# Block transposes and 64x64 tiles in the attention part of a fused attention and MLP kernel

**The chip, the cores, the metric.** One NeuronCore of a Trainium2 chip. The metric is device time in microseconds (us) of one launch. Single runs of one kernel spread by about 2 us here. Names: PE is TensorE's matmul, PEld its weight load, DVE VectorE, ACT ScalarE, POOL GpSimd.

## The reference

Attention with a polynomial sketch, then an MLP with ELU (shapes in comments):

```python
# q, k, v: (batch 4, heads 4, seq 1088, dim 32); S1, S2: (8, 32)
def phi(x):
    a = einsum('rd,bhsd->bhsr', S1, x)
    b = einsum('rd,bhsd->bhsr', S2, x)
    return einsum('bhsi,bhsj->bhsij', a, b).reshape(..., 64)
q_p, k_p = phi(q), phi(k)
kv  = einsum('bhsf,bhsd->bhfd', k_p, v)
z   = sum(k_p, axis=2)
num = einsum('bhsf,bhfd->bhsd', q_p, kv)
den = einsum('bhsf,bhf->bhs', q_p, z)[..., None] + 1e-6
x   = (num / den) -> (4352, 128)
h   = x @ w_in                        # (128, 2048)
out = where(h > 0, h, exp(min(h, 0)) - 1) @ w_out
```

w_in, w_out, S1 and S2 come as float64; the kernel rebuilds float32 values from their words. Everything is computed in float32; a float32 matmul shows as two PE instructions.

## The kernel before

The 4352 rows are cut into 68 half tiles of 64, in groups of 8 (the last, group 8, has 4). The MLP of a group runs in 8 steps: 4 h instructions, ELU on ACT and DVE, and two steps later 4 o instructions. Groups 0 and 1 are interleaved while the weights are converted, so steps 0 to 15 are theirs; group g from 2 on starts at step 8g. In a step, PE does h, then the attention pieces planned for that step ("extras"), then o of two steps earlier. The attention of each group must be ready before its first step. Parts that matter (cuts marked):

```python
def q1(g, ...):               # sketches: queries held (128x128), sketch streamed
    for i in range(n):
        nc.tensor.matmul(p[:, i * 96:i * 96 + 96], qT[b][:, t:t + 2, :], SW[:, b])   # cut
    nc.scalar.copy(abw[g], p)                                                        # cut
def q4(g):                    # outer products, transposed 128x128 on PE
    for hh in range(2):
        ...
                nc.tensor.transpose(p[:, o:o + P], qp[g][:, r:r + 2], ident[:])
        nc.scalar.copy(qpT[g][:, 2 * hh:2 * hh + 2, :nh, :], p)
def q5(g, ...):               # times kv, tiles of 64 rows x 32 columns
    ...
    nc.tensor.matmul(xp[w][D * h:D * h + D, ...], kvS[64 * w:64 * w + 64, b, h, :],
                     qpT[g][64 * w:64 * w + 64, h, ...], tile_position=(64 * w, D * h))
def KA(b, gi):                # kv: outer products held (64 columns), v streamed (33 with the ones)
    ...
    nc.tensor.matmul(kv[64 * hp:64 * hp + 64, g2, :n], kp[:rows, j, h],
                     vt[b][:rows, h * KT + i, :], tile_position=(0, 64 * hp))        # cut
```

Of the kernel before, what the change touches and what calls it, by code (L numbers as in the profile page):

```python
# [27 lines left out]
def kernel(  # L28
# [18 lines left out]

    nc = tc.nc
# [20 lines left out]
    vt = [const.tile([P, VN + D], F32, name="v0")]  # L69
    vt += [const.tile([P, H * KT, D + 1], F32, name=f"v{b}") for b in range(1, B)]  # L70
    kT = [const.tile([FD, NT, 64], F32, name=f"kT{b}") for b in range(B)]
# [8 lines left out]
    def load_v(b, engs=(nc.sync, nc.sync)):  # L80
        for u, eng in enumerate(engs):
            t0, t1 = u * KT, min(NT, u * KT + KT)
            r = slice(64 * u, 64 * u + 64)
            src = v[b].rearrange("h (y t) d -> y h t d", t=NT)[:, :, t0:t1, :]
            if b == 0:
                eng.dma_start(vt[b][r, :VN].rearrange("p (h t d) -> p h t d", h=H, t=KT)[:, :, :t1 - t0, :], src)
            else:
                for h in range(H):
                    eng.dma_start(vt[b][r, h * KT:h * KT + t1 - t0, :D], src[:, h])
# [113 lines left out]
    for b in range(1, B):  # L203
        nc.gpsimd.memset(vt[b][:, :, D:], 1.0)
# [42 lines left out]

    Sab = const.tile([FD, H, 2 * R], F32, name="Sab")
    SW = const.tile([FD, B, H, 3, R], F32, name="SW")
    keep_warm(3)  # L250
    sps = psum.tile([P, 512], F32, name="sps", tag="aux")
# [3 lines left out]
    for b in range(B):  # L255
        nc.gpsimd.tensor_copy(SW[:, b, :, :2, :].rearrange("p h x r -> p h (x r)"), Sab[:])

# [6 lines left out]
    kvS = const.tile([P, B, H, D], F32, name="kvS")  # L264
    kv_ps, feats, zms, abps = {}, {}, {}, {}

    def KF(b, p2=None):

        p = psum.tile([P, 512], F32, name="abp", tag="aux")
        if p2 is None:  # L270
            p2 = psum.tile([P, 512], F32, name="abp2", tag="aux")
        where = [(p, 64 * i) if b or i < 4 else (p2, 64 * i - 256) for i in range(8)] + [(p2, 448)]
        for i in range(KT):
            to = where[i][0][:, where[i][1]:where[i][1] + 64]
            for u in range(2 if i + KT < NT else 1):
                nc.tensor.matmul(to[64 * u:64 * u + 64, :], kT[b][:, u * KT + i, :],  # L276
                                 Sab[:].rearrange("p h y -> p (h y)"),
                                 skip_group_check=True, tile_position=(0, 64 * u))
        abps[b] = [where[i] for i in (0, 4, 8)]

# [15 lines left out]
    def KA(b, gi):  # L296

        kp, rows = feats.pop((b, gi))
        n = 2 * D if b == 0 else D + 1
        if gi == 0:  # L300

            kv_ps[b] = psum.tile([P, 4, 2 * D], F32, name="kv", **(dict(tag="aux") if b == 1 else dict(tag="o1", bufs=1)))
        kv = kv_ps[b]
        for j, i in enumerate(KG[gi]):
            for g2 in range(2):
                for hp in range(2):
# [3 lines left out]
                                     _ap(vt[b][:rows, off:off + D], [[VN - off, 2], [1, D]]) if b == 0 else  # L310
                                     vt[b][:rows, h * KT + i, :],
# [3 lines left out]
    def KC(b):  # L315

        kv = kv_ps[b][:, :2, :D + 1]
        if b == 0:
            for hp in range(2):
                r = slice(64 * hp, 64 * hp + 64)  # L320
                nc.scalar.copy(kvz[0][r, :, hp, :], kv[r])
        else:
            kvz[b] = work.tile([P, 2, 2, D + 1], F32, name="kvz", tag="kvz")
            nc.scalar.copy(kvz[b][:, :, 0], kv)

    def KZ1(b):

        zms[b] = work.tile([P, 2, 2, R], F32, name="zm", tag="zm")
        z_ = kvz[b][:, :, :, D] if b == 0 else kvz[b][:, :, 0, D:]
        nc.gpsimd.tensor_mul(  # L330
            zms[b][:], _ap(z_, [z_.ap[1], z_.ap[2] if b == 0 else [0, 2], [0, R]]),
            _ap(zmask[:], [[0, 2], [R, 2], [1, R]]))

    def KZ2(b):
# [3 lines left out]
        nc.vector.tensor_mul(SW[:, b, :, 2, :], wps[:, :H * R].rearrange("p (h i) -> p h i", h=H),  # L338
                             _ap(bmask[:], [[1, H], [0, R]]))

    def KS(b):

        for w in range(2):
            for hp in range(2):
                nc.gpsimd.tensor_copy(kvS[64 * w:64 * w + 64, b, hp::2, :],
                                      kvz[b][64 * hp:64 * hp + 64, :, hp if b == 0 else 0, :D])
# [10 lines left out]
    def half_tile(g, i, u):  # L357
        return divmod(8 * g + (2 * i + u if g < NQ - 1 else u * qn[g] + i), NT)
# [10 lines left out]
    def q1(g, tag="aux", small=False, b_k=None):  # L369

        n = qn[g]
        p = psum.tile([P, 512], F32, name="abwp", tag=tag, bufs=2 if tag == "aux" else 1)
        for i in range(n):
            (b, t), (b1, t1) = half_tile(g, i, 0), half_tile(g, i, 1)
            if (b1, t1) == (b, t + 1) and not small:
                nc.tensor.matmul(p[:, i * 96:i * 96 + 96], qT[b][:, t:t + 2, :].rearrange("p t s -> p (t s)"),  # L376
                                 SW[:, b].rearrange("p h x r -> p (h x r)"), skip_group_check=True)
                continue
            for u, (b, t) in enumerate(((b, t), (b1, t1))):
                nc.tensor.matmul(p[64 * u:64 * u + 64, i * 96:i * 96 + 96], qT[b][:, t, :],  # L380
                                 SW[:, b].rearrange("p h x r -> p (h x r)"),
                                 skip_group_check=True, tile_position=(0, 64 * u))
        if b_k is not None:
            KF(b_k, p)

        abw[g] = work.tile([P, H * 4, 3 * R], F32, name="abw", tag="abw", bufs=2)
        nc.scalar.copy(abw[g][:, :H * n, :].rearrange("p (h t) y -> p h t y", h=H),  # L387
                       p[:, :n * 96].rearrange("p (t h y) -> p h t y", t=n, h=H))
        if b_k is not None:
            KF_out(b_k)  # L390

    def q2(g, parts=1):
        m = H * qn[g]
        x = abw[g][:, :m, :]
        pw = pws[g % 2]
        nc.vector.tensor_mul(pw[:, :m, :R], x[:, :, R:2 * R], x[:, :, 2 * R:])
# [15 lines left out]
    def q1_first():  # L412
        p = psum.tile([P, 512], F32, name="abqp", tag="aux")
        for i in range(4):
            for u in range(2):
                b, t = half_tile(0, i, u)
# [29 lines left out]
    def q5_first(xps):  # L446
# [21 lines left out]
        for tt in range(2):  # L468
# [4 lines left out]
            if tt == 0:  # L473
                q1(1)

    def q4(g):

        nh = qn[g] // 2
        qpT[g] = work.tile([P, H, 2, P], F32, name="qpT", tag="qpT", bufs=2)
        for hh in range(2):  # L480
            p = psum.tile([P, 512], F32, name="qtp", tag="aux")
            for h2 in range(2):
                for m in range(nh):
                    o = (h2 * nh + m) * P
                    r = (2 * hh + h2) * qn[g] + 2 * m
                    nc.tensor.transpose(p[:, o:o + P], qp[g][:, r:r + 2].rearrange("p t i j -> p (t i j)"), ident[:])  # L486
            nc.scalar.copy(qpT[g][:, 2 * hh:2 * hh + 2, :nh, :],  # L487
                           p[:, :2 * nh * P].rearrange("p (h m s) -> p h m s", h=2, m=nh))

    def q5(g, between=False):  # L490
        nh = qn[g] // 2
        xp = [psum.tile([P, 512], F32, name="xps", tag="aux") for _ in range(2)]

        parts = {0: [], 1: []}
        for w in range(2):
            for m in range(nh):
                b, b1 = (half_tile(g, 2 * m + w, u)[0] for u in range(2))
                if b != b1:
                    parts[w] += [(b, m, 1, slice(0, 64)), (b1, m, 1, slice(64, P))]
                elif parts[w] and parts[w][-1][0] == b and parts[w][-1][3] == slice(0, P):  # L500
                    parts[w][-1] = (b, parts[w][-1][1], parts[w][-1][2] + 1, slice(0, P))
                else:
                    parts[w] += [(b, m, 1, slice(0, P))]
        for h in range(H):
            for w in range(2):
                for b, m0, m, s in parts[w]:
                    nc.tensor.matmul(xp[w][D * h:D * h + D, :nh * P].rearrange("p (m s) -> p m s", s=P)[:, m0:m0 + m, s],  # L507
                                     kvS[64 * w:64 * w + 64, b, h, :], qpT[g][64 * w:64 * w + 64, h, m0:m0 + m, s],
                                     skip_group_check=True, tile_position=(64 * w, D * h))
        xg[g] = work.tile([P, 512], F32, name="xg", tag="xg", bufs=2)  # L510
        if not between:
            q5_out(g, xp)
        return xp

    def q5_out(g, xp):
        nh = qn[g] // 2
        to = xg[g][:, :2 * nh * P].rearrange("p (m w s) -> p w m s", w=2, s=P)
        nc.scalar.copy(to[:, 0], xp[0][:, :nh * P].rearrange("p (m s) -> p m s", s=P))  # L518
        nc.vector.tensor_copy(to[:, 1], xp[1][:, :nh * P].rearrange("p (m s) -> p m s", s=P))
# [72 lines left out]
    def fin_last():  # L592
# [5 lines left out]
        for u, eng in enumerate((nc.sync, nc.scalar)):  # L598
            b, t = half_tile(g, 0, u)
# [3 lines left out]
    keep_warm(2, 192)  # L603
# [7 lines left out]
    x0 = x0_eps()  # L611
# [9 lines left out]
    KS(0)  # L621
# [3 lines left out]
    RC(1)  # L625
    for c in range(2):
# [3 lines left out]
    RA(2)  # L630
    RB(2)
    q4(1)
# [3 lines left out]
    x1 = q5(1, True)  # L636
    elu_a(0, 1, 0, (0,))
    q5_out(1, x1)
    keep_warm(1)
    elu_a(0, 1, 0, (1,))  # L640
    elu_a(0, 1, 1)
# [115 lines left out]
```

## Time and profile before

| | before |
|---|---|
| median of the first 3 runs | 291.74 us (290.99 to 293.24) |
| the profiled run | 290.04 us, span of the core 288.3 us |
| busy in the span | PE 281.5, ACT 187.1, DVE 166.4, POOL 17.1 us |
| on the chain that ended last | PE 87%, of it h 36% and o 35% of the span |

PE is the bound; h and o are the MLP itself, which the change does not touch. The chain in order of time is the view to read: its pieces are spaced as the engine really moved. Its lines stand in the prediction.

### The profile page before, as it was taken

What the parts mean: (1) busy time and instruction counts of PE and PEld (TensorE: products, weight loads), DVE (VectorE), ACT (ScalarE), POOL (GpSimd) and SP (SyncE); (2) the same over time, 40 slices, a digit from 0 to 9 for tenths busy, and PEclk for the clock granted to TensorE, in tenths of its full rate; (3) what the DMA queues carried; (4) which work ended last, traced back from release to release, by engine and by line L of the source; (5) the groups of instructions that cost most, each with busy time, mean ns of one, the idle gap of its engine ahead of it and who ended that gap; (6) DMA issues with size and microseconds to landing.
All of it is one profiled execution on the core that took longest, in us unless ns stands there. A gap on an engine that the chain in (4) does not pass through costs nothing.

```text
span 288.3 us, 3955 instructions
## 1 busy us (share of the span) xinstructions
PE 281.5 (98%) x1432; PEld 147.5 (51%) x1432; DVE 166.4 (58%) x298; ACT 187.1 (65%) x357; POOL 17.1 (6%) x49
## 2 busy tenths in 40 slices
PE   7999999999999999999999999999999999999994
PEld 5864355445544745454444554445445544444694
DVE  5897999794864483546344443563442654354442
ACT  2468787567584665646776658665766676668682
POOL 3100003533000101000000000000000000000000
PEclk9999999999999999999999999999999999999999
DMA  6997993200004000002001000020002000100020
GB/s 175 338 276 189 201 227 35 77 0 0 2 1 68 7 0 3 0 6 35 0 0 23 13 2 0 2 35 2 0 0 36 2 2 0 25 11 0 7 32 18
DMA packets 37282, 13.36 MB, mean 46 GB/s; under 512 B 31760, under 2 KB 35472, under 8 KB 37264
## 3 DMA queue, kind: packets, MB, share of 16 engines
q1 hardware_dynamic: 36752, 12.66, 19.7%
q10 hardware_dynamic: 512, 0.46, 0.5%
q8 instruction: 11, 0.18, 0.3%
q14 instruction: 7, 0.06, 0.1%
HBM read 10.88 MB, written 2.23 MB: 45 GB/s over the span
## 4 chain that ended last, share of the span: by engine, by line
PE 87%; DVE 5%; DMA 2%; ACT 2%; POOL 1%; SPq 1%; issue 1%; POOLq 0%; DVEq 0%; ACTq 0%
PE h L529 36%; PE o L566 35%; PE kv L309 3%; PE ol L589 2%; PE xps L507 2%; PE qtp L486 2%; DMA v<-in_v_dram 2%; PE abwp L376 1%; DVE gg L553 1%; PE abp L276 1%; PE abwp L380 1%; ACT e L547 1%; PE x0ps L456 1%; DMA raw_s<-in_S_dram 1%; DVE raw L120 1%
## 5 line engine op out<-in xcount | busy, mean ns | idle before, releaser
L553 DVE SCALAR_TENSOR_TENSOR gg<-e,h 128x512 f32<-128x512 f32 (+1 forms) x144 | 93.1, 656 | 105.5 <-ACT e L547 105.4
L529 PE MATMUL h<-xg,W 128*128 128x512 f32 (+1 forms) x284 | 126.9, 569 | 0.6 <-DVE W L128 0.5
L566 PE MATMUL o<-gg,W 128*128 128x512 f32 x256 | 121.9, 598 | 0.0
L545 ACT ACTIVATE e<-h 128x512 f32<-128x512 f32 (+1 forms) x144 | 81.3, 565 | 34.1 <-PE h L529 30.3
L547 ACT ACTIVATE e<-e 128x512 f32<-128x512 f32 (+1 forms) x144 | 87.3, 606 | 4.5
L529 PEld LDWEIGHTS h<-xg,W 128*128 128x128 f32 x284 | 53.3, 190 | 62.9 <-issue 55.0
L566 PEld LDWEIGHTS o<-gg,W 128*128 128x128 f32 x256 | 46.6, 190 | 50.2 <-issue 48.9
L487 ACT COPY qpT<-qtp 128x512 f32<-128x512 f32 (+1 forms) x16 | 8.1, 560 | 15.5 <-PE qtp L486 15.5
L387 ACT COPY abw<-abwp 128x384 f32<-128x384 f32 (+1 forms) x8 | 3.7, 458 | 18.4 <-PE abwp L376 8.7
L261 DVE TENSOR_TENSOR kp<-ab 128x1024 f32<-128x1024 f32 (+1 forms) x12 | 12.1, 1044 | 0.1
L309 PEld LDWEIGHTS kv<-v,kp 128*64 128x64 f32 (+1 forms) x288 | 9.1, 137 | 1.7 <-ACT e L545 0.8
L309 PE MATMUL kv<-v,kp 128*64 128x33 f32 (+3 forms) x288 | 9.8, 224 | 0.0
L107 ACT ACTIVATE W<-W,ebias 128x256 uint32<-128x256 uint32 (+1 forms) x11 | 6.6, 597 | 4.8 <-DVE W L102 4.6
L407 DVE TENSOR_TENSOR qp<-an,abw 128x1024 f32<-128x1024 f32 (+1 forms) x9 | 9.3, 1047 | 0.3
L486 PEld LDWEIGHTS qtp<-ident,qp 128*128 128x128 f32 x60 | 7.1, 141 | 4.2 <-issue 4.2
L518 ACT COPY xg<-xps 128x256 f32<-128x256 f32 (+1 forms) x8 | 2.9, 359 | 9.1 <-PE xps L507 9.1
L589 PEld LDWEIGHTS ol<-W,gg 128*128 128x128 f32 x64 | 8.1, 192 | 0.3
L589 PE MATMUL ol<-W,gg 128*128 128x128 f32 x64 | 8.1, 275 | 0.0
L486 PE MATMUL qtp<-ident,qp 128*128 128x128 f32 x60 | 7.9, 272 | 0.0
L507 PE MATMUL xps<-qpT,kvS 64*32 64x256 f32 (+2 forms) x176 | 6.7, 316 | 0.4 <-ACT qpT L487 0.4
L125 POOL TENSOR_TENSOR raw<-raw,tiny 128x512 f32<-128x512 f32 x4 | 4.2, 1044 | 42.8 <-DVE raw L120 38.8
L507 PEld LDWEIGHTS xps<-qpT,kvS 64*32 64x32 f32 x176 | 3.2, 105 | 6.3 <-ACT e L547 5.3
(89 smaller groups left out, 129.9 us busy)
## 6 DMA issues: line engine op xcount, KB each, us to landing
raw<-in_moe_w_in_dram SPq DMA_DIRECT2D x8, 256.0 KB, 6.1
raw<-in_moe_w_out_dram SPq DMA_DIRECT2D x8, 256.0 KB, 6.5
hd_k<-in_k_dram SPq DMA_DIRECT2D x3, 544.0 KB, 6.5
hd_q<-in_q_dram SPq DMA_DIRECT2D x3, 544.0 KB, 3.8
out_dram<-ob SPq DMA_DIRECT2D x40, 32.0 KB, 1.6
v<-in_v_dram SPq DMA_DIRECT2D x12, 72.0 KB, 6.3
v<-in_v_dram SPq DMA_DIRECT2D x12, 64.0 KB, 3.3
hd_k<-in_k_dram SPq DMA_DIRECT2D x1, 288.0 KB, 3.5
```

What stands on the lines that cost most here:

```text
L261: nc.vector.tensor_mul(dst, _ap(a_, list(a_.ap[1:]) + [[0, R]]), _ap(b_, [b_.ap[1], [0, R], b_.ap[2]]))
L309: nc.tensor.matmul(kv[64 * hp:64 * hp + 64, g2, :n], kp[:rows, j, h].rearrange("p i j -> p (i j)"), _ap(vt[b][:rows, off:off + D], [[VN - ...
L407: nc.vector.tensor_mul(qp[g][:, h], _ap(a_, list(a_.ap[1:]) + [[0, R]]), _ap(b_, [b_.ap[1], [0, R], b_.ap[2]]))
L486: nc.tensor.transpose(p[:, o:o + P], qp[g][:, r:r + 2].rearrange("p t i j -> p (t i j)"), ident[:])
L487: nc.scalar.copy(qpT[g][:, 2 * hh:2 * hh + 2, :nh, :], p[:, :2 * nh * P].rearrange("p (h m s) -> p h m s", h=2, m=nh))
L507: nc.tensor.matmul(xp[w][D * h:D * h + D, :nh * P].rearrange("p (m s) -> p m s", s=P)[:, m0:m0 + m, s], kvS[64 * w:64 * w + 64, b, h, :], ...
L529: nc.tensor.matmul(hs[g, cp][c][:, :n], W[:, cp, c * P:c * P + P], xg[g][:, :n])
L545: nc.scalar.activation(e, hs[g, cp][c][:, :n], RELU, scale=-1.0)
L547: nc.scalar.activation(e, e, EXP, scale=-1.0)
L553: nc.vector.scalar_tensor_tensor(gs[g, cp][:, c, :n], es[g, cp][:, c, :n], -1.0, hs[g, cp][c][:, :n], op0=ADD, op1=MAX)
L566: nc.tensor.matmul(ops[g][:, :n], W[:, cp, (2 + c) * P:(3 + c) * P], gg[:, c, :n], start=(first and c == 0), stop=(last and c == 1))
L589: nc.tensor.matmul(ops[g][i][:], gg[:, c, i * P:i * P + P], W[:, cp, (2 + c) * P:(3 + c) * P], start=(first and c == 0), stop=(last and c ...
```

## The change

The intent is to spend less PE time on attention in groups 2 to 8 and in the keys of batches 1 to 3. The sketch is held and the queries streamed, in four 64x64 tiles; transposes of 32x32 blocks on DVE replace 128x128 transposes on PE; q5 of one group and q1 of the next share one visit. On the key side v is held (32 columns) and the outer products streamed, four heads on four column tiles. z comes from a product of the two sketches. Cut to its core:

```diff
+    def KA_late(b):
+        for i in range(KT):
+            for h in range(H):
+                nc.tensor.matmul(kv[32 * h:32 * h + 32, :R * R], vt[b][...], kp[i // 5][...],
+                                 tile_position=(0, 32 * h), ...)
+            nc.tensor.matmul(kv[c:c + 32, R * R:R * R + H * R], ab[:, 0, i], ab[:, 1, i],
+                             tile_position=(0, c), ...)
...
+    def q1(g, ps):
+        for e in range(2):
+            for g2 in range(2):
+                    nc.tensor.matmul(ps[g2][64 * e:64 * e + 64, 256 + 64 * k:...], SWp[r, b], qT[b][r, t:t + m, :],
+                                     tile_position=(64 * g2, 64 * e), ...)
+    def q1_out(g):
+            nc.vector.transpose(abw[g][...], ps[g2][:, 256:256 + 32 * n])
...
+    def q4(g):
+        nc.vector.transpose(qpT[g][...], qp[g][...])
+    def q5(g, ps):
+        for f in range(2):
+            for g2 in range(2):
+                for e in range(2):
+                        nc.tensor.matmul(ps[e][64 * g2:64 * g2 + 64, ...], kvp[r, b, f, g2], qpT[g][r, ..., f, :],
+                                         tile_position=(64 * e, 64 * g2), ...)
...
-    keep_warm(2, 192)
+    x0 = x0_eps()              # moved ahead of the first key work
...
+            ((3, 5, (6, 7), 8, 10, 9), (11, 12, (13, 14), 19, 20, 21), (17, 18, (20, 21), 22, 24, 25)), 1):
+    # steps of: transpose of k, sketch, two outer products, kv, z, transpose of q
```

## The prediction

> **What bounds the kernel now.** I read the page's first two parts, then the stretches between chosen times, then the chain that ended last in order of time, then the groups by shape, and last the vector engine's own order of time.
>
> ```profile
> PE 281.5 (98%) x1432; PEld 147.5 (51%) x1432; DVE 166.4 (58%) x298; ACT 187.1 (65%) x357; POOL 17.1 (6%) x49
> ...
> PE   7999999999999999999999999999999999999994
> ...
> DVE  5897999794864483546344443563442654354442
> ```
>
> ```profile
> 28.00:46.00 18.00, 17.45 (x71) 7.63 (x70) 17.62 (x32) 14.65 (x29) 2.40 (x2) 1.00 0.97 191
> ...
> 160.00:260.00 100.00, 100.00 (x346) 46.27 (x346) 47.17 (x79) 68.35 (x123) 0.00 (x0) 1.00 0.06 9
> ```
>
> TensorE is busy throughout. In the stretches the columns are length, then busy time (and instructions) of PE, PEld, DVE, ACT and POOL. From 160 us on only PE is full. From 28 to 46 us DVE is full too (17.62 of 18.00 us), because the weights are converted there. So a PE instruction saved late is saved time; one saved early may meet DVE. "Busy" alone doesn't say what an attention block costs, as ends are modelled; the chain does, since each piece there is time from one start to the next:
>
> ```profile
> 92.89 0.81 PE abwp L380 x16
> 93.70 0.93 PE abp L276 x32
> 94.74 2.19 PE kv L309 x71
> 96.94 1.91 PE o L566 x4
> 98.85 1.72 PE h L529 x4
> ...
> 104.22 0.88 PE qtp L486 x8
> 105.10 1.72 PE o L566 x4
> 106.81 1.72 PE h L529 x4
> 108.53 0.59 PE xps L507 x16
> 109.12 2.34 PE kv L309 x72
> 111.47 1.91 PE o L566 x4
> ```
>
> A step of the main loop is four h and four o instructions, 3.44 us. Between them stand the extras: abwp projects the queries, qtp transposes their outer products, xps multiplies by kv, abp and kv are the key side. An o after a block of small tiles takes 1.91 us, 0.19 more than the plain 1.72; after qtp (full 128x128 array) it takes 1.72. The main matmuls are not touched, so the question is what the extras sum to, and whether the new chain on DVE arrives in time.
>
> **What the Trainium skill says.**
> - "TensorE: Matmul & The Clock Gate", Part 3 (packing small matmuls): matmuls in different tiles of the array run together, starts about 4 ns apart. The trace agrees where each tile gets few instructions: the 16 xps instructions (64x32 tiles, 256 columns) took 0.59 us. Two such passes on one tile are 427 ns (half of the 1.72/4 = 0.43 us of a 512-column instruction, twice); 0.16 is filling.
> - The same page, the section on LDWEIGHTS: the load time goes with the columns, P/1.2 ns: 53 ns for 64, 27 for 32. The trace fits: 8 abwp instructions with 128-column loads took 0.86 us, 108 ns each, though their 96 columns stream in 80. The kv instructions (64-column loads, 33 columns streamed, two tiles) took 2.34/72 = 32.5 ns, 65 per tile: nearer the load than the 27 ns of stream.
> - "TensorEngine Tiling (Array Packing)", Key Properties: changing the tiling mode drains the engine. The 0.19 us on the next o is this, as far as this trace shows.
> - The first page again, on the issue gap: starts never fall below about 25 ns. That would hurt many-instruction blocks. The trace is undecided: 24 xps instructions at 141.12 us took 0.61 us (25 ns each), yet 16 cannot be told from the tile limit.
>
> **The change, part by part.**
>
> *Queries, groups 2 to 8.* Before: abwp on PE, copy on ACT, qtp on PE (8 transposes) with two ACT copies, xps, two copies. After: q1 holds the sketch (64x64) and streams the queries, 8 instructions on four tiles; a DVE transpose of 32x32 blocks brings it back; the qtp transposes become one DVE transpose; q5 is 16 instructions of 256 columns on four tiles; q5 of one group and q1 of the next share one visit. Per tile q1 has two passes, 427 ns, q5 four, 853; with 0.16 of filling and 0.19 of drain a visit is 1.63 us. Boundary groups, cut in more pieces, add about 0.5 in all.
> Before, from the chain, a plain group is 0.86 + 0.03 + 0.87 + 0.59 + 0.19 = 2.54 us. All seven groups, read off the chain: abwp 5.6, qtp 5.7, xps 5.0, ten drains 1.9, so 18.2. After: six visits 9.8, less 0.2 for the short last q1, plus the lone first q1 (0.43 + 0.16 + 0.19 = 0.78), the lone last q5 (0.78) and 0.5: 11.7. Saved 6.5.
>
> *Keys of batches 1 to 3.* Before: abp 1.20 + 2 x 0.93 = 3.1, kv 2.34 + 2.19 + 2.34 = 6.9, z matmuls 3 x 0.13 = 0.4 us; with two drains not shared with a query block, 10.8. After, the sketch matmul is 16 instructions of 288 columns on eight tiles, two passes per tile: 0.48 + 0.16 + 0.19 = 0.83 each, 2.5. The outer products are streamed (64 columns, 53 ns) against v held (32 columns), four heads on four tiles, 90 instructions: per row block two passes of some 58 to 66 ns on each tile and a z piece of 27 to 60, so 145 to 190 ns, nine times, plus 0.15: near 1.5 us, 4.9 for three with two unshared drains. I choose 1.5 rather than the 2.4 that a 25 ns floor would make. The z product and two more transposes cost 0.45 each, 1.35. Sum 8.75; saved 2.0.
>
> PE extras: 29.0 to 20.5, **minus 8.5 us**.
>
> *The start.* The eps product (1.08 us on the chain before kv) moves ahead into idle PE time. But the first outer product of the queries ends on DVE only at 11.46 us and the transposes after it hardly move: I give 0.1, and 0.1 for the earlier copy of the second group: minus 0.2. The fewer v transfers (2 per batch instead of 8) win nothing: no DMA wait but 0.4 us of q and 0.6 of the sketches is listed.
>
> *New work on DVE.* ACT loses two 0.59 copies and one of 0.48 per group and takes one of 0.37 from DVE; ACT was not the bound. DVE gains per group a 1024-element transpose (1.2 us by the 1.31 of the 1088-element ones) and two PSUM transposes of 256 (0.45 each). After step 24 DVE has half of its time free; it costs nothing. At step 13, though, work heaps up:
>
> ```profile
> 70.55 0.28 DVE L396 TENSOR_TENSOR pw<-abw 128x128 f32<-128x128 f32 x1
> 70.87 0.30 DVE L398 TENSOR_REDUCE den<-pw 128x16 f32<-128x144 f32 x1
> 71.21 0.25 DVE L399 RECIPROCAL den<-den 128x16 f32<-128x16 f32 x1
> 71.50 0.29 DVE L401 TENSOR_TENSOR an<-abw,den 128x128 f32<-128x128 f32 x1
> 71.82 1.23 DVE L407 TENSOR_TENSOR qp<-an,abw 128x1024 f32<-128x1024 f32 x1
> 72.96 1.22 DVE L261 TENSOR_TENSOR kp<-ab 128x1024 f32<-128x1024 f32 x1
> ```
>
> These were steps apart from the key work. Now step 13 gives DVE a key outer product of 1280 elements (1.6, scaled from the 1.22), two gg (1.2), two transposes (0.9) and the chain above up to qp (2.4 to the start of the next): 6.0 us against a PE step of 4.2. Step 14 adds 1.2 + 1.2 and the transpose of qp (1.2) in 3.44. Following it from the start of h in step 13: qp ends near 7.1, the second key product 8.4, gg 9.6, the transpose 10.8; PE reaches q5 at 4.2 + 3.44 + 1.72 = 9.4. **A wait of about 1.5 us** in step 15, once.
>
> In steps 5 to 8 DVE takes on two transposes of 288 (0.9) but the key products come in other steps; by the same walk gg stays inside the slack that four h buffers give. I count no loss there.
>
> Sum: 291.74 - 8.5 - 0.2 + 1.5 = 284.5. I put **284.0 us**, because the walk to step 15 lets nothing overlap on DVE, where the trace has starts up to 0.1 us before the end of the one ahead.
>
> **Rivals.**
> 1. *Instruction issue takes over on PE.* Kv becomes 90 instructions instead of 72; at 25 to 28 ns each it takes 2.25 to 2.6 us and saves nothing. For: the 24 xps instructions at 25 ns each and 40 of group 6 in 1.12 us (28 each). Against: the 16 loads of a plain xps start within 0.2 us. It would add 3 us: 287.
> 2. *DVE becomes the bound.* Some 1.7 us more DVE work per group, and steps 2 to 9 are full. If every DVE microsecond added before step 16 (about 5) turned into PE waiting, the gain would shrink to 4 or 5 us: 287. Against: later DVE waits for ACT 105 us in all.
> 3. *No wait at step 15* and no drains between q5 and q1: 282, or 281 with kv at 1.2 us.
> 4. *The four 64x64 tiles don't run together* (eight and two tiles do in the trace, four nowhere): a visit would grow by over 2 us and the kernel be slower. Unlikely.
>
> **Range and chances.** The kv duration (1.2 to 2.5 us, three times) and the wait at step 15 (0 to 2.5) are the two wide terms, plus the sum of drains (some 1 us): 280.5 to 287.5. Faster by over 2% means below 285.9: most of the range. Faster 0.80, same 0.19, slower 0.01.
>
> **What would show it.** The new qps blocks of a plain group should take 1.4 us and the next o 1.91; kv of a late batch 1.5 us; kfps 0.64; the chain should show one wait of PE for the DVE transpose of qp near step 15, and no wait of q5 or h later. Qtp and the copies behind it should be left for the first two groups alone. ACT busy should fall, DVE busy rise by about 15 us while PE stays full. The prediction is wrong if kv is above 2 us, if DVE holds PE up more than once, or if the four tiles serialise.

## The result

The changed kernel took 283.32 us (median of 4 runs, 282.73 to 284.6) against 291.37 us for the kernel before (4 runs with one more beside it). The ratio is 0.9724, 95% interval 0.9658 to 0.979: faster by 2.8%. A ratio here is the mean time of one kernel's fast runs over that of the other's of the same rounds, so not quite the ratio of the medians. The time was predicted 0.7 us too high.

The page of the changed kernel, busy time by engine, and PE's busy tenths in 40 slices of the span:

```profile
PE 273.7 (97%) x1348; PEld 138.4 (49%) x1348; DVE 178.7 (63%) x319; ACT 179.8 (64%) x337; POOL 20.9 (7%) x55
...
PE   8999998999979999999999999999999999999994
```

DVE rose by 12.3 us and ACT fell by 7.3. PE now shows a 7 in slice 12 (77.6 to 84.6 us): a wait that was not there. The chain of the changed kernel (start us, length us, what; the z pieces between those of kv are too short to be listed):

```profile
93.72 1.72 PE h L661 x4
95.70 0.46 PE kvl L340 x23
96.78 1.91 PE o L698 x4
...
138.58 1.08 PE qps L627 x16
139.66 0.44 PE qps L492 x8
140.10 1.91 PE o L698 x4
```

Read it by the gaps between the large pieces. h ends at 93.72 + 1.72 = 95.44 and o starts at 96.78, so the whole of kv for batch 2 took 1.34 us for its 90 instructions, 15 ns each; the old one took 2.34 for 72. A visit of the queries is 1.08 (q5) + 0.44 (q1) = 1.52 us, and the o behind it takes 1.91 as before. The qtp, abwp and xps pieces are gone after the second group.

The wait in step 15, in order of time on PE and on DVE:

```profile
75.70 1.88 PE L661 MATMUL h<-xg,W 128*128 128x512 f32 x4
79.07 1.16 PE L627 MATMUL qps<-qpT,kvp 64*64 64x64 f32 x24 [1.49 <-DVE qpT L617]
```

```profile
74.22 1.23 DVE L520 TENSOR_TENSOR qp<-an,abw 128x1024 f32<-128x1024 f32 x1
75.36 1.22 DVE L282 TENSOR_TENSOR kpl<-abk 128x1024 f32<-128x1024 f32 x1
76.50 1.28 DVE L685 SCALAR_TENSOR_TENSOR gg<-e,h 128x512 f32<-128x512 f32 x2
77.69 1.24 DVE L617 STREAM_TRANSPOSE qpT<-qp 128x1024 f32<-128x1024 f32 x1
```

The bracket says that PE was idle 1.49 us until the DVE transpose of qp ended. On DVE the pieces stand without a gap: the second key product and two gg lie between qp and its transpose.

A second wait, with DVE, POOL and PE in order of time:

```profile
44.18 1.48 DVE L282 TENSOR_TENSOR kpl<-abk 128x1280 f32<-128x1280 f32 x1
...
44.34 2.22 POOL L122 TENSOR_TENSOR raw<-raw,tiny 128x512 f32<-128x512 f32 x1 [19.23 <-DVE raw L117]
...
47.98 1.98 PE L661 MATMUL h<-xg,W 128*128 128x512 f32 x4 [1.15 <-POOL W L123]
```

POOL's first multiply (its second, 1.29 us, follows), which took 1.04 us in the kernel before, took 2.22 beside a DVE product of two SBUF tiles, and h of step 8 waited 1.15 us for the converted weights.

Last, the start. The sketches of the first keys in time order on PE, first in the profile before and then in that of the changed kernel:

```profile
6.32 1.15 PE L276 MATMUL abp<-Sab,kT 128*64 128x64 f32 x32 [0.17 <-DVE kT L237]
```

```profile
7.48 2.08 PE L298 MATMUL abp<-Sab,kT 128*64 128x64 f32 x33
```

The same instructions take nearly twice as long in the second trace, because PE still ran at its slow clock. The record of the granted clock in the trace file shows it: its first entry, full clock, stands at 4.4 us before and at 10.6 us in the changed kernel, behind these sketches. (The PEclk row of the page does not show it; what precedes the first entry is left out there.) The first h, at 16.26 us before, came at 17.81, 1.55 us later. From the first h to the end, before took 288.3 - 16.26 = 272.0 us and the changed kernel 282.1 - 17.81 = 264.3, so 7.7 less. This stretch, "from the first h", repeats to 0.1 us in five profiles of kernels that do the same from there on (264.3 each), while the first h moves between 16.5 and 18.6 us. I use it below wherever a difference is under 2 us. It still holds the tail from the last matmul to the last output. That took 3.6 to 3.7 us in these five, but 4.0 in the profiles of before, e3b and e8 and 3.5 in that of e4; e3b and e8 change nothing near the end, so I take this as a matter of the single run, whose reason I don't know. The stretch from the first h to the end of the last matmul is free of it: 268.0 us before, 260.6 in the changed kernel, 7.4 less (7.35 before rounding).

### The profile page after: what moved, and what is told of

It is laid out like the page before. It is cut to its first block, busy times and chain, and to the rows that moved or that the text cites. A ratio compares the mean times of both kernels' runs of the same rounds, so it can differ in the third digit from the quotient of the medians.

```text
span 282.1 us, 3800 instructions
## 1 busy us (share of the span) xinstructions
PE 273.7 (97%) x1348; PEld 138.4 (49%) x1348; DVE 178.7 (63%) x319; ACT 179.8 (64%) x337; POOL 20.9 (7%) x55
## 4 chain that ended last, share of the span: by engine, by line
PE 87%; DVE 8%; issue 1%; ACT 1%; POOL 1%; POOLq 0%; DVEq 0%
PE h L661 37%; PE o L698 36%; PE ol L721 3%; PE qps L627 2%; DVE gg L685 2%; PE kvl L340 1%; PE idle L221 1%; DVE kp L282 1%; PE qps L492 1%; POOL raw L122 1%; PE x0ps L569 1%; DVE raw L117 1%; PE h L668 1%; PE x0ps L554 1%; DVE W L112 1%
## 5 line engine op out<-in xcount | busy, mean ns | idle before, releaser
L627 PE MATMUL qps<-qpT,kvp 64*64 64x256 f32 (+3 forms) x136 | 7.4, 339 | 1.5 <-DVE qpT L617 1.5
L617 DVE STREAM_TRANSPOSE qpT<-qp 128x1024 f32<-128x1024 f32 (+1 forms) x7 | 8.1, 1161 | 0.0
L282 DVE TENSOR_TENSOR kpl<-abk 128x1280 f32<-128x1280 f32 (+1 forms) x6 | 8.1, 1346 | 0.0
L627 PEld LDWEIGHTS qps<-qpT,kvp 64*64 64x64 f32 x136 | 4.7, 132 | 6.6 <-issue 3.1
L502 DVE STREAM_TRANSPOSE abw<-qps 128x256 f32<-128x256 f32 (+1 forms) x14 | 5.2, 407 | 2.0 <-ACT xg L639 2.0
L117 DVE SCALAR_TENSOR_TENSOR raw<-raw 128x256 f32<-128x256 uint32 (+1 forms) x11 | 6.0, 549 | 0.3
L112 DVE SCALAR_TENSOR_TENSOR W<-raw,W 128x256 uint32<-128x256 uint32 (+1 forms) x11 | 5.9, 541 | 0.0
L705 DVE STREAM_TRANSPOSE ob<-o 128x512 f32<-128x512 f32 x8 | 5.7, 710 | 0.1
L639 ACT COPY xg<-qps 128x256 f32<-128x256 f32 x12 | 3.9, 373 | 2.8 <-PE qps L492 2.8
L123 POOL TENSOR_TENSOR W<-raw,W 128x512 f32<-128x512 f32 x4 | 5.4, 1342 | 0.3
```

What stands on the lines that cost most here:

```text
L112: nc.vector.scalar_tensor_tensor(d, hi, 0x80000000, d, op0=AND, op1=OR)
L117: nc.vector.scalar_tensor_tensor(lo.bitcast(F32), lo, 2.0 ** -32, raw[:, :, 1], op0=MUL, op1=ADD)
L282: nc.vector.tensor_mul(dst, _ap(a_, list(a_.ap[1:]) + [[0, R]]), _ap(b_, [b_.ap[1], [0, R], b_.ap[2]]))
L627: nc.tensor.matmul(ps[e][64 * g2:64 * g2 + 64, 64 * k:64 * (k + m)], kvp[r, b, f, g2].rearrange("p c d -> p (c d)"), qpT[g][r, n * g2 + 2 ...
```

## Experiments

All ran against the kernel before. Runs e0 to e3 were one call, e4, e5, e6 and e3b another, e7, e8 and e9 a third, on another chip. All gave correct results. First h to the end and to the last matmul are from the profiled run of each.

| run | median us | ratio to before | first h, us | from the first h, us | of it to the last matmul, us |
|---|---|---|---|---|---|
| e0_after (changed kernel) | 283.10 | 0.9720 | 17.82 | 264.3 | 260.6 |
| e1_lead | 284.02 | 0.9749 | 18.35 | 264.3 | 260.6 |
| e2_ko | 283.00 | 0.9711 | 18.37 | 263.1 | 259.5 |
| e3_kp7 | 282.37 | 0.9702 | 18.44 | 263.4 | 259.7 |
| e3b_nopool | 282.86 | 0.9709 | 16.59 | 263.7 | 259.7 |
| e4_oldkeys | 286.35 | 0.9838 | 17.09 | 267.1 | 263.6 |
| e5_split | 286.34 | 0.9832 | 17.82 | 266.3 | 262.7 |
| e6_dve | 283.10 | 0.9723 | 16.50 | 264.3 | 260.6 |
| e7_best | 280.94 | 0.9656 | 18.41 | 261.8 | 258.1 |
| e8_best2 | 281.36 | 0.9659 | 17.09 | 262.2 | 258.1 |
| e9_after (changed kernel) | 284.10 | 0.9753 | 18.56 | 264.3 | 260.7 |

My theory: the gain is PE time of the attention pieces, queries and keys; part is given back in two waits that DVE causes. Rivals: the gain comes from elsewhere (the start, or DVE and ACT work moved), or new limits (instruction rate, DVE) ate the rest.

### e0_after: the yardstick

No edit.

> The changed kernel again, unaltered, as the yardstick for the runs beside it. Both theories expect about 283.3 us, 0.972 of before. If the length of the lead-in (first h matmul at 17.8 us in the profile of the changed kernel, 16.26 in that of before) hangs on when TensorE's clock warms up and not on the code, this profile may show another lead-in, 1 to 1.5 us shorter, and the single times should fall in two groups about 1.5 us apart.

The six runs lay between 282.58 and 283.92 us, and the profile repeated both waits. The first h was again at 17.82. In e9 the same kernel had it at 18.56, and e6, whose start is untouched, at 16.50. The kernel before does it too: 11 runs had spans of 288.2 to 288.4 us (three) or 289.8 to 290.3 (eight), and the profile from which I predicted, 288.3, was one of the short kind. So the start differs from run to run, and one profile of each kernel must not be compared there. The clock records of the profiles go with it: full clock came at 4.4 to 4.9 us where the first h came at 16.3 to 16.6 (before, e6, e3b), at 10.3 to 10.6 where it came at 17.8 (the changed kernel, e0, e5), and at 12.6 to 13.0 where it came at 18.4 to 18.6 (e2, e3, e7, e9). In e4 and e8 it came at 4.4 and 4.6, was halved again from 7.8 and 8.0 to 11.2 and 11.4, and the first h came at 17.09.

### e1_lead: the start of the kernel before

```diff
-    keep_warm(1, 160)
...
-    x0 = x0_eps()
+    keep_warm(2, 192)
...
     q1_first()
+    x0 = x0_eps()
```

> The changed kernel with the lead-in of before: the eps product back behind the first query projection, the two idle matmuls of 192 columns back, the extra one of 160 columns gone. Theory A (the new lead-in costs time, since the early eps product keeps TensorE at its slow start longer): first h near 16.3 us instead of 17.8 and the time 1.5 us lower than the changed kernel of the same call, near 281.8. Theory B (it is the phase of the clock's warm-up, which changes from run to run): no difference in the mean beyond 0.5 us. Theory C (my prediction: the new lead-in saves 0.1 us): 283.4, same as the changed kernel.

Theory A is out: with the old start the first h came at 18.35 us, not 16.3, and the time did not fall: the mean was 283.93 against 283.22 us for e0. The means alone settle no more, since the changed kernel itself had 283.95 in the third call. The clock records do: in e1 full clock came at 10.4 us, in e0 at 10.3, in e5 at 10.5 and in the first profile of the changed kernel at 10.6, and with the new start the first h came at 17.81 to 17.82 in all three. So with the clock as late as this the new start is worth 0.5 us, on the evidence of one trace of the old one. With an early clock no run compares the two.

### e2_ko: two key products moved out of steps 13 and 14

```diff
-            (11, 12, (13, 14), 19, 20, 21)
+            (11, 12, (16, 17), 19, 20, 21)
```

> The changed kernel with the two outer products of batch 2's keys moved from steps 13 and 14 to 16 and 17 (needed in step 19). My theory: the 1.49 us wait of TensorE for the transposed qp at 79.07 us comes from DVE work heaped up in steps 13 and 14, 2.6 us of it these two products; it goes away, and the time falls by 1.3 to 1.5 us, to about 281.9. Rival: DVE is short of time in the whole stretch up to step 20, and the wait turns up again later (at kv of batch 2 or at h): the time stays within 0.4 us.

The group of q5 instructions (last columns: busy us, mean ns, idle before them us and its releaser):

```profile
L627 PE MATMUL qps<-qpT,kvp 64*64 64x256 f32 (+3 forms) x136 | 7.4, 339 | 0.4 <-DVE qpT L617 0.4
```

The wait fell from 1.5 to 0.4 us and the stretch from the first h from 264.3 to 263.1, 1.2 us. The median hardly moved (283.00); the profiled run of it started late, its first h at 18.37 us. The heap of DVE work is the cause, and the wait did not turn up again. I had the size slightly high: 0.4 is left. In this trace DVE still runs without a gap from 72.1 us to 78.4 us, the end of the transpose of qp: one gg, two transposes, the chain to qp, two more gg. In e7, where that chain starts a step earlier, the rest of the wait goes too.

### e3_kp7 and e3b_nopool: the wait for POOL

```diff
-            ((3, 5, (6, 7), 8, 10, 9)        # e3_kp7
+            ((3, 5, (7, 7), 8, 10, 9)
-        at(n, RC, i, i > 6)                  # e3b_nopool
+        at(n, RC, i, i > 7)
```

> The changed kernel with the first outer product of batch 1's keys moved from step 6 to step 7, where the second one is. Theory: the 1.15 us wait of h for the weights that GpSimd converts (at 47.98 us) comes from this product running beside GpSimd's multiply, which then took 2.22 us instead of the 1.04 that it took before; with the product later the multiply takes about 1.1 us, h doesn't wait, but kv in step 8 waits some 0.5 us for the second product, so 0.3 to 1.1 us less, near 282.7. Rival: GpSimd's multiply is slow for another reason: it stays near 2.2 us and the wait stays.

> The changed kernel with the last conversion step of the weights of step 8 on DVE instead of GpSimd. Theory (h of step 8 waits for GpSimd): DVE needs 0.69 us for what takes GpSimd 2.22 + 1.29, so the 1.15 us wait goes; gg of step 6 comes 0.7 us later, so 0.5 to 1.1 us less, 282.4. Rival: DVE is full there, and the added work makes h wait for gg instead: 283.2 or more.

The chain of e3_kp7:

```profile
45.05 1.04 POOL raw L122
46.18 1.49 POOL W L123
```

With the DVE product one step later, POOL's multiply took 1.04 us again, the wait for POOL shrank to 0.2 and the stretch from the first h by 0.9 us. Taking POOL off the path (e3b) won 0.6 by that stretch, but its tail was 0.3 us longer; to the last matmul both won 0.9. So the DVE product beside it slows POOL, and this cost 0.9 us net. The size follows from who starts first. In e4 below, POOL's multiply again starts behind a DVE product:

```profile
42.74 1.22 DVE L287 TENSOR_TENSOR kp<-ab 128x1024 f32<-128x1024 f32 x1
42.97 1.89 POOL L127 TENSOR_TENSOR raw<-raw,tiny 128x512 f32<-128x512 f32 x1 [23.88 <-issue]
```

When POOL started, 0.99 us of the product were left, and its multiply took 0.85 longer than 1.04. In the changed kernel 1.32 us were left (44.18 + 1.48 - 44.34), and it took 1.18 longer. In e3_kp7 it is the other way round: the moved product starts at 46.42, behind POOL's second multiply, of which 1.24 us are left, and takes 2.58 us instead of 1.48, 1.10 longer. So in all three the later of the two lost what was left of the earlier, less 0.14 us.

### e4_oldkeys: queries changed, keys as before

Abridged:

```diff
-        at(n_f, KF_late, b)                  # and KO_late, KA_late, KC_late, KZ_late
+        at(n_f, KF, b)                       # and KO, KA, KC, KZ1, KZ2 of the kernel before
+        late(n_a, KS, b)                     # kv copied to the new layout on POOL
+    # v of batches 1 to 3 with its ones column and 8 transfers, as before
```

> Half of the change undone: keys of batches 1 to 3 as in the kernel before (kp held, v streamed, z from the ones column, copies on GpSimd into the new kv layout), queries as in the changed kernel. From the chains of both kernels the key part should cost 3 x (2.34 - 1.35) for kv + 3 x (0.93 - 0.65) for the sketches - 3 x (0.39 - 0.13) for z = 3.0 us more TensorE time than the changed kernel: 286.2. My prediction had the keys saving 2.0: 285.2. Rival: the keys save nothing (more instructions, 90 for 72, eat up the shorter loads): 283.3. The rest of the gain against before, 5 to 6 us, is then the queries'.

It took 286.35 us, and 263.6 from the first h to the last matmul: 3.0 more than the changed kernel (2.8 with the tail, which was 0.2 shorter). Two pieces of its chain:

```profile
48.42 2.34 PE kv L402 x72
...
64.92 1.19 PE abp L303 x34
```

The rival is out: more instructions did not eat the gain. But the right total hides two errors of mine. A sketch piece on its own takes 1.19 us, not 0.93. So, with the queries changed, the new keys save 3 x (2.34 - 1.34) + 3 x (1.19 - 0.65) - 3 x (0.39 - 0.14) = 3.9 us of PE time; and the wait for POOL (1.1 us) was absent in e4 (POOL was done in time there, though its multiply was slowed too), while the one for q5 was 0.3 longer. 3.9 - 1.1 + 0.3 = 3.1, near the 3.0 measured. The queries alone gave 268.0 - 263.6 = 4.4 us net, with e4's own wait of 1.8 us for q5 in it.

### e5_split: q5 and q1 in separate visits

```diff
-        at(n5, queries, g, g + 1 if g + 1 < NQ else None)
+        at(n5, queries, g, None)
+        if g + 1 < NQ:
+            at(n5 + 1, queries, None, g + 1)
```

> The changed kernel with q1 of the next group moved out of the visit of q5 into a visit of its own one step later, for groups 3 to 8: the same instructions, six more changes between the full array and 64x64 tiles. Theory (each visit pays about 0.16 us of filling and 0.19 of drain on the next o): 6 x 0.35 = 2.1 us more, 285.3; each lone q1 takes about 0.6 us and the o after it 1.91. Rival (cost goes with instructions and columns alone): no change, 283.2.

The chain of e5:

```profile
143.97 0.59 PE qps L492 x8
144.56 1.91 PE o L698 x4
```

From the first h it took 266.3 us, 2.0 more: 0.33 per added visit, of which 0.19 is the longer o and about 0.14 the filling (0.59 alone against 0.44 to 0.49 behind q5). The profiled runs of both kernels, with the same first h, agree: 285.93 and 283.92. The medians differ by 3.2. The spans of e5's four runs, 284.1 to 285.0 us, less 266.3 put their first h at 17.8 to 18.7 us, inside the range seen, so the rest fits a late start; it is not shown run by run.

### e6_dve: six idle DVE transposes more

```diff
+        if g > 2:
+            nc.vector.transpose(spare[...], qp[g][...])
```

> The changed kernel with the transpose of qp done a second time, into a spare tile that nobody reads, for groups 3 to 8: 6 more DVE instructions, some 6.7 us of DVE busy time. Theory (DVE has slack after step 20, so the new DVE work is free there): no change, 283.2 within 0.4. Rival (DVE is close to the bound, so its new work costs time): 2 to 6 us more.

No change: 283.10 us and 264.3 from the first h. After step 20 DVE work of this size is free, so the new DVE work is free there too.

### e7_best and e8_best2: both waits removed

```diff
-            ((3, 5, (6, 7), 8, 10, 9), (11, 12, (13, 14), 19, 20, 21)
+            ((3, 5, (7, 7), 8, 10, 9), (11, 16, (17, 18), 19, 20, 21)
-    at(13, queries, None, 2)
+    at(12, queries, None, 2)
-        n1, n2, n4, n5 = (13, 13, 14, 15) if g == 2
+        n1, n2, n4, n5 = (12, 12, 13, 15) if g == 2
```

e8_best2 keeps (6, 7) and finishes the weights of step 8 on DVE, as e3b does.

> The changed kernel with both waits attacked: batch 1's first key product in step 7, batch 2's sketch moved to step 16 and its products to 17 and 18, and group 2's first projection and quotients one step earlier (12) with the transpose of qp in 13. Theory: the waits of 1.49 us (q5) and 1.15 us (h for GpSimd's weights) both go, against some 0.3 us of new waiting: 2.0 to 2.4 us less than the changed kernel from the first h to the end (262.0 for its 264.1), 281.0 in the mean. Rival: DVE in steps 9 to 20 is so full that a wait turns up at another place; then less than 1.2 us is won.

> As e7_best, but batch 1's first key product stays in step 6 and the weights of step 8 are finished on DVE, not GpSimd. From the single tests (0.9 us won by moving the product, 0.6 by taking GpSimd off) it should be 0.3 us slower than e7_best: 262.3 from the first h to the end, 281.3 in the mean.

> The changed kernel beside the two candidates: mean 283.2, 264.1 us from the first h to the end, with the first h between 16.7 and 18.6 us.

The chain of e7 at step 15:

```profile
76.33 1.09 PE qps L627 x14
77.42 0.43 PE qps L492 x8
```

h before it started at 74.62 and takes 1.72 us, so q5 follows at once. From the first h e7 took 261.8 us, 2.5 less than the changed kernel, and e8 262.2; to the last matmul both took 258.1, and the means of 6 runs, 281.11 and 281.18 us, can't be told apart. So the 0.3 us that I expected between them came from the tail of e3b, not from its edit. Both beat both kernels: e7 is 3.4% faster than before. e9 gave 264.3 from the first h (264.1 expected) and a mean of 283.95 (283.2 expected).

## Why the prediction was right

**The PE sum.** I had 29.0 us of attention pieces going to 20.5. Reading the changed chain the same way gives 19.7: queries 11.6 (predicted 11.7), sketches of keys 2.5 (2.5), kv 3 x 1.34 + 2 x 0.19 = 4.4 (4.9), z 3 x 0.39 = 1.2 (1.35). So 9.3 us saved for my 8.5. The 29.0 is itself too low: it leaves out that an o behind a z piece took 1.80 us, 0.08 more, three times, and gaps on the chain such as that from 94.63 to 94.74 us. By the starts in the timeline the pieces went from 29.7 to 19.9, which is 9.8 us saved: 6.7 on the queries, 3.0 on the keys for my 2.0 (the 3.9 of e4 are more, because two of the old sketches no longer share a visit with a query projection there). That the queries' 11.6 met my 11.7 is partly luck: a shared visit took 1.52 + 0.19 = 1.71 us, not 1.63, and the 0.5 us for the cut boundary groups did not come (q5 and q1 together took 1.49 us in one such visit, at 109.01 us, and 1.52 in the plain one). The four 64x64 tiles do run together: q5's 16 instructions of 256 columns took 1.02 to 1.08 us, where one after the other they would need 16 x 0.215 = 3.4 (0.215 is half of the 0.43 us of a 512-column instruction). Rival 4 is out.

**Kv and the instruction rate** (rival 1). I chose 1.5 us and it took 1.34. At 15 ns per instruction, the 25 ns floor that I quoted from the skill doesn't bind between tiles.

**The wait at step 15.** Predicted "about 1.5 us", measured 1.49. Here the walk through DVE's order was worth its length. Counted from the start of h in step 13 (68.03 us in the trace) it had qp end at 7.1, the second key product at 8.4, gg at 9.6 and the transpose at 10.8; they ended at 7.4, 8.6, 9.8 and 10.9. e2 showed that the two key products cause the wait. But then I took 0.5 us off the sum (284.5 to 284.0) because starts on DVE overlap a little. The wait came in full, so that step closer to the result was luck. Rival 3, no wait, was what the schedule could have had; e7 has it.

**DVE in steps 5 to 8** (the step "I count no loss there"). This was wrong. I looked only at gg and the four h buffers, not at GpSimd, which shares its work on the weights with DVE. The Trainium skill, "SBUF — State Buffer", section Who interferes with whom, says that a DVE instruction with two SBUF inputs contends with a GpSimd instruction that reads SBUF. This trace agrees: 1.04 us alone, 2.22 beside the product. It cost 1.15 us of waiting, 0.9 net by e3. A sign was there: in the kernel before, the h of step 8 already started right behind POOL's second multiply (44.64 + 1.43 = 46.07, h at 46.12). I had written that the prediction is wrong if DVE holds PE up more than once. By the profile this second wait is POOL's, but a DVE product made it, so that sign half came. (The other two, kv above 2 us and tiles one after the other, did not.)

**The start.** I gave it 0.2 us of gain. The two profiles show 1.55 us of loss, but the clock records show that full clock came 6.2 us later in the second (4.4 and 10.6 us), and with the same start code e6 and e3b have the early clock, while most runs of the kernel before have the longer span. What the edit itself does is 0.5 us of gain when the clock is late (e1) and unknown when it is early.

**Accounts, from the first h to the last matmul.** Added up from start to start on PE, the attention pieces with their filling and drains went from 29.7 to 19.9 us: -9.8. Main matmuls that started late added 0.9 us before (0.7 and 0.2 of h waiting for weights) and 3.3 after (0.5 and 1.3 in front of h, 1.6 in front of q5): +2.4. Sum -7.4; measured 268.0 to 260.6, -7.4. The steps from the first h to the first o took 8.56 us in both kernels, so the work moved about there on ACT and DVE gave nothing. The other 0.3 of the 7.7 us is the tail, which can't be put down to the change. That the total was only 0.7 us off comes in part from a saving on PE (9.8 for 8.5) and a wait for POOL (1.1 more for none) that I both put too low.

## What to carry to other kernels

When one engine is the bound, sum its extra pieces by the starts on the chain, not by busy times, and then walk the other engines' order at the step where the new work heaps up; averages by engine showed neither of the two waits. Small matmuls pay by the visit (about 0.33 us here) and by the passes on one tile, not by the instruction. Before two profiles are compared, check whether the start of both ran at the same clock, and count from a point behind it.

## What the Trainium skill lacked or had wrong

- "TensorE: Matmul & The Clock Gate" says that starts never come closer than about 25 ns. Across four column tiles that are used again and again, 90 kv instructions ran at 15 ns each (1.34 us). The page's own 4 ns between tiles fits better; the floor would need the words "on one tile".
- The same page has the warm-up vary by about 500 ns from run to run. With one and the same start code full clock came at 4.7 us in one run (e6) and at 13.0 in another (e9), and the first h at 16.50 and 18.56 us. It calls the ramp below 1% of a kernel; these 2.06 us are 0.7%, but a quarter of this change's gain.
- "TensorEngine Tiling (Array Packing)" says that a change of mode drains the engine and gives no cost. Here an added visit cost 0.33 us, of which 0.19 fell on the next full-array matmuls.
- "SBUF — State Buffer" says of DVE and GpSimd that the second one to issue blocks until the first finishes, but gives no times for a two-input product. Here GpSimd's multiply went from 1.04 to 2.22 us, while the DVE product, which started 0.16 us earlier, took 1.48 us, as it does with GpSimd idle (1.48 at 100.08 us). In three traces the later one lost what was left of the earlier less 0.14 us (1.18 of 1.32, 0.85 of 0.99, 1.10 of 1.24), so a little less than a full block.
